# Attention and expert layers on one core: store order, ranks of the front, casts of v on other engines, and a new order of the last unit

## The chip, the cores and the metric

One core of one Trainium2 chip runs the whole program. The metric is device time in microseconds (us). The kernel before takes 982.17 us (median of 4 runs). Time quotients below are the mean time of one kernel's runs over that of the other's runs of the same rounds, so not quite the ratio of the medians that stand beside them. The span in a profile is about 1.8 us shorter than the time of the same run.

Short names: PE is the tensor engine, DVE the vector engine, ACT the scalar engine, POOL GpSimd, SP the engine that issues most transfers. In the lines, kin, qin and vin are loaded inputs, ek and eq their exponentials, tk and tq phi of k and q, vv is v in fp16, w a weight tile, h the result of layer 1 after relu, acc the summed output. A fused pair is the two SCALAR_TENSOR_TENSOR instructions of DVE that make one tk or tq. An eviction is the instruction of DVE or ACT that takes a finished product from PE.

## The reference

```python
# q, k, v: [8, 8, 576, 64]; x: [4608, 512]; 8 experts; w1: [8, 512, 1024], w2: [8, 1024, 512]
q_p, k_p = phi(q), phi(k)                    # phi(x) = (x if x > 0 else exp(x) - 1) + 1
kv  = einsum('bhsd,bhse->bhde', k_p, v);  z = k_p.sum(2)
x   = einsum('bhsd,bhde->bhse', q_p, kv) / (einsum('bhsd,bhd->bhs', q_p, z) + 1e-6)   # then to [4608, 512]
P   = exp(x @ w_gate - max);  8 rounds of normalising rows and columns
out = sum over e of  P[:, e:e+1] * (relu(x @ w1[e]) @ w2[e])
```

## The kernel before

It has three stages. The **front** handles 16 attention blocks (two per batch element): load k, q, v; exponentials, clamps and sums for phi; products kv, qt (transpose), den, num, xt. Beside it run nine **plain units** (expert 0, 512 rows each: 32 products hq of layer 1, 32 products ye of layer 2). They fill PE while the blocks come in. Then follow 63 units of experts 1 to 7, all but the last in a form with seven block products in place of eight; in the last expert's last unit only layer 1 has that form. Its block products are called a1 to a7 and b1 to b7, the layer-2 ones y1 to y7.

Nothing is scheduled by hand. A small list scheduler runs while the program is written: each task has planned durations, dependencies and a rank, and the order of instructions in each engine's stream is whatever it decides. This order is then part of the program; what the profiles add is the waits.

```python
    def run(self):                      # cut: the scheduler
        ...
                for t in lst:           # of the tasks that can start soonest, the lowest rank goes first
                    r = slot(t)
                    if r is not None and r <= te + 1e-9 and (pick is None or (t["prio"], t["id"]) < (pick["prio"], pick["id"])):
                        pick = t
```

The parts that the change touches:

```python
    p_e = S_.pool(2)
    ...
        tvv.append(fadd(("pool", 1.3), f_v, deps=[ta, tin["v"]],      # cast of v to fp16, 128 x 1152
                        use=[gvv, gin["v"]], prio=pr))
    ...
        ti = add(("sp", 0.2), f_raw, deps=deps + [t_close], prio=0.0)  # raw x to memory, then the sums
        ...
        ti = add(("sp", 0.1), f_st, deps=[last], use=[gt_], prio=0.0)
    ...
    w_t[1] = load_w1(1, prio=0.0, after=110.0) + load_w2(1, prio=0.0, after=115.0)
    order = "y1 y5 y2 y6 a7 y3 y7 a4 b1 b5 y4 b6 b3 b2 b7 A1 A5 b4 A6 A3 A2".split()
    chain = []
    for u in range(NG - 1, E * NG + 1):
        for n in order:
            ...
```

The softmax here doesn't subtract the row's maximum and nothing guards it: scores larger than these inputs give would overflow.

Of the kernel before, what the change touches and what calls it, by code (L numbers as in the profile page):

```python
# [10 lines left out]
FP32 = mybir.dt.float32  # L11
FP16 = mybir.dt.float16
# [110 lines left out]
def kernel(  # L123
# [10 lines left out]
    nc = tc.nc  # L134

    B, H, S, D = q.shape
# [4 lines left out]
    P = 128  # L141
# [37 lines left out]
    kvz_t = [fp.tile([P, 2, 2, D + 1], FP16, tag=f"kvz{i}", name=f"kvz{i}", bufs=1) for i in range(2)]  # L179

    p_in = {n: S_.pool(2) for n in "kvq"}
    p_e = S_.pool(2)
    p_t = {n: S_.pool(2) for n in "kq"}
    p_vv, p_kvz, p_qpT, p_xn, p_rden = (S_.pool(2) for _ in range(5))
    p_att, p_hq, p_h = S_.pool(2), S_.pool(2), S_.pool(2)
# [27 lines left out]
    def load_w1(e, **kw):  # L213
        return load_w(moe_w1, "w1", p_w1, [[F, P], [F * P, NDT], [1, F]], 2, e, **kw)

    def load_w2(e, **kw):
        return load_w(moe_w2, "w2", p_w2, [[DM, P], [DM * P, NFT], [1, DM]], 1, e, **kw)
# [9 lines left out]
    w_last, in_prev = [None], [None]  # L227
    front_ids = []
    xt_done = {}
    vcast = {}  # L230

    def fadd(*a, **kw):
        t = add(*a, **kw)
        front_ids.append(t)
        return t

    def att(b, g):
# [22 lines left out]
        for nm in "kq":  # L260
            ge = S_.grp(p_e)
            gt[nm] = S_.grp(p_t[nm])

            def f_e(_, ge=ge, nm=nm):
                ge["tile"] = fp.tile([P, 2, NJ, D], FP16, tag="e", name="e" + nm)
                nc.scalar.activation(out=ge["tile"], in_=gin[nm]["tile"], func=AF.Exp)

            def f_t(e, g_=gt[nm], nm=nm):
                g_["tile"] = fp.tile([P, NJ, 2, D], FP16, tag="t" + nm, name="t" + nm)
                g_["on"] = e  # L270
                if e == "act":
                    nc.scalar.add(out=g_["tile"].rearrange("p j r d -> p r j d"), in_=gin[nm]["tile"], add=1.0)  # L272

            def f_m(_, ge=ge, g_=gt[nm], nm=nm):
                nc.vector.tensor_scalar(out=ge["tile"], in0=ge["tile"], scalar1=1.0, scalar2=None, op0=ALU.min)
                o = g_["tile"].rearrange("p j r d -> p r j d")
                if g_["on"] == "act":
                    nc.vector.tensor_tensor(out=o, in0=o, in1=ge["tile"], op=ALU.max)
                else:
                    for r in range(2):  # L280
                        nc.vector.scalar_tensor_tensor(out=o[:, r], in0=gin[nm]["tile"][:, r], scalar=1.0,  # L281
                                                       in1=ge["tile"][:, r], op0=ALU.add, op1=ALU.max)
            te = fadd(("act", 1.17), f_e, deps=[tin[nm]], acq=[ge], use=[gin[nm]], prio=pr)
            tt_ = fadd({"dve": 0.6, "act": 1.17}, f_t, deps=[tin[nm]],
                       acq=[gt[nm]], use=[gin[nm]], prio=pr)
            tph[nm] = fadd(("dve", 1.35), f_m, deps=[te, tt_], use=[ge, gt[nm], gin[nm]], prio=pr)
# [5 lines left out]
        ta = fadd(("none", 0.0), f_va, deps=[tin["v"]], acq=[gvv], prio=pr)  # L292
        def f_v(e):
            copy(e, gvv["tile"][:, :, :, 0:D], gin["v"]["tile"])
        tvv.append(fadd(("pool", 1.3), f_v, deps=[ta, tin["v"]],
                        use=[gvv, gin["v"]], prio=pr))
        vcast[n] = tvv[0]
        gkv, gz = [S_.grp(p_ye[2]), S_.grp(p_ye[3])], S_.grp(p_kvz)

        def f_kv(_):  # L300
# [160 lines left out]
        return add(("dve", 0.8), f_p, deps=last, prio=-200.0)  # L461

    nc.vector.memset(ones_t, 1.0)
    warm = const.tile([P, 512], FP16, tag="warm", name="warm")
    nc.vector.memset(warm, 0.0)

# [20 lines left out]
        nc.vector.memset(kvz_t[i], 0.0)  # L487
    att(0, 0)
    att(0, 1)
    w_t = {0: load_w1(0, prio=-290.0, parts=2, deps=[vcast[0]])}  # L490
    for b in range(1, B):
        att(b, 0)
        att(b, 1)
# [26 lines left out]
    def layer1(e, g):  # L520
        gw1, tw1, gw2, tw2 = w_t[e]
        bs = range(512 * g // S, (512 * g + 511) // S + 1)
        xd_ = [xt_done[(b, c)] for b in bs for c in range(NDT)]
        th = []
        gh = S_.grp(p_h)

        def f_ha(_):
            gh["tile"] = hpool.tile([P, NFT, 512], FP16, tag="h", name="h")
        tha = add(("none", 0.0), f_ha, deps=[prev_hq[0]], acq=[gh], prio=g - 400.0)
        for f in range(NFT):  # L530
            ghq = S_.grp(p_hq)

            def f_hq(_, f=f, ghq=ghq):
                ghq["tile"] = hqp.tile([P, 512], FP32, tag="hq", name="hq")
                for c in range(NDT):
                    nc.tensor.matmul(ghq["tile"], lhsT=gw1["tile"][:, c, ts(f, P)], rhs=xT[:, c, ds(512 * g, 512)],  # L536
                                     start=(c == 0), stop=(c == NDT - 1))

            def f_rl(_, f=f, ghq=ghq):
                nc.scalar.activation(out=gh["tile"][:, f, :], in_=ghq["tile"], func=AF.Relu)  # L540
            t1 = add(("pe", 0.87), f_hq, deps=[tw1[f // 4], prev_hq[0]] + xd_, acq=[ghq], use=[gw1],
                     prio=g + 0.1 * f + 0.35)
            prev_hq[0] = t1
            x_users.append(t1)
            th.append(add(("act", 0.6), f_rl, deps=[t1, tha], use=[ghq, gh], prio=g - 400.0))
        return gh, [th, th]

    def x_blocks(g):
        bs = range(512 * g // S, (512 * g + 511) // S + 1)
        deps = [xt_done[(b, c)] for b in bs for c in range(NDT)]  # L550
        t0 = 512 * g
        gt_ = S_.grp(p_xst)

        def f_raw(_):
            nc.sync.dma_start(out=xd[g][:, 0:512].rearrange("p (c t) -> p c t", c=2), in_=xT[:, 0:2, t0:t0 + 256])
            nc.sync.dma_start(out=xd[g][:, 512:1536].rearrange("p (c t) -> p c t", c=2), in_=xT[:, 2:4, t0:t0 + 512])
        ti = add(("sp", 0.2), f_raw, deps=deps + [t_close], prio=0.0)
        out_ = [add(("dma", 1.0), lambda _: None, deps=[ti], prio=0.0, lat=2.6)]
        last = None
        for i in range(4):  # L560
            def f_T(_, i=i):
                if i == 0:
                    gt_["tile"] = accp[1].tile([P, 4, 2, 256], FP16, tag="xst", name="xst")
                T = gt_["tile"]
                b11, b12 = xT[:, 0:2, t0:t0 + 256], xT[:, 0:2, t0 + 256:t0 + 512]
                b21, b22 = xT[:, 2:4, t0:t0 + 256], xT[:, 2:4, t0 + 256:t0 + 512]
                a0, a1 = [(b12, b11), (b22, T[:, 0]), (b22, b12), (b21, T[:, 1])][i]
                nc.vector.tensor_tensor(out=T[:, i], in0=a0, in1=a1, op=ALU.subtract)
            last = add(("dve", 0.42), f_T, deps=deps + [t_close, last], acq=[gt_] if i == 0 else [], use=[gt_],
                       prio=g - 8.0)  # L570
            x_users.append(last)

        def f_st(_):
            nc.sync.dma_start(out=xd[g][:, 1536:NXB], in_=gt_["tile"].rearrange("p i c t -> p (i c t)"))
        ti = add(("sp", 0.1), f_st, deps=[last], use=[gt_], prio=0.0)
        out_.append(add(("dma", 1.5), lambda _: None, deps=[ti], use=[gt_], prio=0.0, lat=2.6))
        x_users.append(out_[0])
        return out_

    def x_load(e, g):  # L580
# [114 lines left out]
    def unit_plain(e, g, gW=None, tW=None):  # L695
# [4 lines left out]
        for tt in range(4):  # L700
            for half in range(2):
                def f_y(_, half=half, tt=tt):
                    if half == 0:
                        gy[tt]["tile"] = yps.tile([P, 512], FP32, tag=f"ye{tt % 2}", name=f"ye{tt % 2}")
                    for f in range(4 * half, 4 * half + 4):
                        nc.tensor.matmul(gy[tt]["tile"], lhsT=gh["tile"][:, f, ds(P * tt, P)], rhs=gw2["tile"][:, f, :],  # L706
                                         start=(f == 0), stop=(f == NFT - 1))
                ty[tt] = add(("pe", 0.87), f_y, deps=[tw2[half], ty[tt]] + (th[0][4 * half:4 * half + 4] if e == 0 else th[tt // 2]),
                             acq=[gy[tt]] if half == 0 else [], use=[gw2, gh],
                             prio=e * NG + g + 0.1 * (2 * tt + half) + 0.65)  # L710
        for tt in range(4):
            gg = 4 * g + tt

# [148 lines left out]
            for tt in range(4):  # L862
                out_dma(g, tt, [fin_prev[(4 * g + tt, dh)] for dh in range(2)])

    w_t[1] = load_w1(1, prio=0.0, after=110.0) + load_w2(1, prio=0.0, after=115.0)
    xd_done, xs_prev, x_closed = {}, [None], [None]
    pe_id = {}
    for g in range(NG):
# [7 lines left out]
    for e in range(1, E):  # L876
# [3 lines left out]
        for g in range(NG):  # L880
            if e == E - 1 and g == NG - 1:
                unit_plain(e, g, *co[0:2])
            else:
                unit(e, g, *co)
    order = "y1 y5 y2 y6 a7 y3 y7 a4 b1 b5 y4 b6 b3 b2 b7 A1 A5 b4 A6 A3 A2".split()
    chain = []
    for u in range(NG - 1, E * NG + 1):
        for n in order:
            key = (u - 1, n) if n[0] == "y" else (u + 1, n.lower()) if n[0] == "A" else (u, n)
            if key in pe_id:  # L890
                chain.append(pe_id[key])
    for d, k_ in zip(chain, chain[1:]):
        S_.dep(k_, d)
    S_.run()


# [28 lines left out]
```

## Time and profile before

| | us |
|---|---|
| time | 982.17 |
| span in the profile | 982.2 |
| PE idle from 22.5 to 125 us | 8.66 |
| PE idle from 125 to 950 us | 0.1 |
| last unit's first layer-2 product of the unit ahead (y1, 958.88) to the end | 23.3 |

The middle, over 800 us, has no hole. What can be won lies in the first 125 us and in the last 25; the prediction shows the lines. This profile fell on a run of its own of 983.97 us, slower than all four that make the median.

### The profile page before, as it was taken

What the parts mean: (1) busy time and instruction counts of PE and PEld (TensorE: products, weight loads), DVE (VectorE), ACT (ScalarE), POOL (GpSimd) and SP (SyncE); (2) the same over time, 40 slices, a digit from 0 to 9 for tenths busy, and PEclk for the clock granted to TensorE, in tenths of its full rate; (3) what the DMA queues carried; (4) which work ended last, traced back from release to release, by engine and by line L of the source; (5) the groups of instructions that cost most, each with busy time, mean ns of one, the idle gap of its engine ahead of it and who ended that gap; (6) DMA issues with size and microseconds to landing.
All of it is one profiled execution on the core that took longest, in us unless ns stands there. A gap on an engine that the chain in (4) does not pass through costs nothing.

```text
span 982.2 us, 21403 instructions
## 1 busy us (share of the span) xinstructions
PE 962.2 (98%) x8716; PEld 792.7 (81%) x8716; DVE 771.7 (79%) x1561; ACT 563.2 (57%) x1034; POOL 127.9 (13%) x171
## 2 busy tenths in 40 slices
PE   7899999999999999999999999999999999999997
PEld 4455564488888888888888888888888888888885
DVE  6898869967777777777777777777777777777774
ACT  4798754565555555555555555555555555555552
POOL 4111200001111111111111111111111111111110
PEclk9999999999999999999999999999999999999999
DMA  9886953162226312272225322272225322236663
GB/s 318 257 303 239 265 160 140 65 127 77 75 76 142 97 73 76 76 161 76 77 75 137 101 76 75 76 162 76 76 76 137 102 76 76 76 103 168 161 161 98
DMA packets 47029, 121.99 MB, mean 124 GB/s; under 512 B 4177, under 2 KB 18001, under 8 KB 46929
## 3 DMA queue, kind: packets, MB, share of 16 engines
q1 hardware_dynamic: 32128, 99.76, 30.3%
q0 software_dynamic: 14480, 20.33, 11.5%
q8 instruction: 68, 1.11, 0.5%
q10 hardware_dynamic: 320, 0.52, 0.1%
q14 instruction: 33, 0.26, 0.1%
HBM read 119.69 MB, written 17.69 MB: 140 GB/s over the span
## 4 chain that ended last, share of the span: by engine, by line
PE 89%; DVE 1%; ACT 1%; issue 0%
PE ye L809 33%; PE hq L627 23%; PE att L627 11%; PE Zye L627 6%; PE Zye L809 6%; PE ye L706 5%; PE hq L536 4%; PE xt_ps L387 0%; PE kv_ps L306 0%; PE num_ps L371 0%; PE lg_ps L405 0%; DVE tk L281 0%; PE qt_ps L332 0%; ACT tq L272 0%; PE den_ps L347 0%; ACT qpT L221 0%
## 5 line engine op out<-in xcount | busy, mean ns | idle before, releaser
L823 DVE SCALAR_TENSOR_TENSOR acc<-ye,P_sb,acc 128x256 f32<-128x256 f32 x620 | 264.9, 477 | 95.3 <-PE ye L809 77.9
L627 PEld LDWEIGHTS <-W 128*128 128x128 f16 x2016 | 197.1, 98 | 23.7
L809 PEld LDWEIGHTS <-S 128*128 128x128 f16 x1984 | 194.1, 98 | 22.7 <-issue 0.3
L809 PE MATMUL ye<-T,S 128*128 128x256 f16 x1488 | 192.8, 273 | 0.1
L833 POOL TENSOR_TENSOR acc<-acc,st 128x256 f32<-128x256 f32 x124 | 87.5, 725 | 625.6 <-ACT st L830 620.7
L653 ACT ACTIVATE h<-hq 128x512 f16<-128x512 f32 x126 | 76.3, 606 | 160.8 <-PE hq L627 160.8
L627 PEld LDWEIGHTS <-w 128*128 128x128 f16 x1512 | 147.6, 98 | 23.3 <-issue 1.0
L809 PEld LDWEIGHTS <-h 128*128 128x128 f16 x1488 | 145.6, 98 | 16.8
L627 PE MATMUL hq<-xs,W 128*128 128x256 f16 x1008 | 151.2, 273 | 0.0
L627 PE MATMUL att<-xs,W 128*128 128x256 f16 x1008 | 151.2, 272 | 0.0
L627 PE MATMUL hq<-xs,w 128*128 128x256 f16 x1008 | 140.7, 272 | 0.8 <-DVE h L656 0.8
L782 DVE TENSOR_TENSOR S<-h 128x1024 f16<-128x1024 f16 x124 | 85.4, 688 | 57.9 <-ACT h L653 57.9
L656 DVE CUSTOM_DVE_ANT_0 h<-att,s 128x512 f16<-128x512 f32 x126 | 86.7, 688 | 13.1 <-ACT s L643 13.1
L830 ACT ACTIVATE st<-Zye,P_sb 128x256 f32<-128x256 f32 x124 | 52.1, 471 | 78.0 <-PE Zye L809 78.0
L643 ACT COPY s<-hq 128x512 f32<-128x512 f32 x126 | 75.0, 595 | 36.7 <-PE hq L627 36.7
L650 ACT ACTIVATE h<-Zye 128x512 f16<-128x512 f32 x126 | 75.2, 597 | 35.1 <-PE Zye L627 35.1
L656 DVE CUSTOM_DVE_ANT_0 h<-hq,s 128x512 f16<-128x512 f32 x126 | 86.5, 686 | 0.8 <-PE hq L627 0.7
L639 ACT COPY Zye<-hq 128x512 f32<-128x512 f32 x126 | 73.3, 581 | 16.3 <-PE hq L627 16.3
L706 PE MATMUL ye<-w,h 128*128 128x512 f16 x320 | 77.6, 379 | 0.9 <-DVE acc L223 0.9
L627 PE MATMUL Zye<-xs,w 128*128 128x256 f16 x504 | 75.6, 273 | 0.0
L647 ACT COPY s<-att 128x512 f32<-128x512 f32 x126 | 74.5, 591 | 0.0
L536 PE MATMUL hq<-xT,w 128*128 128x512 f16 x288 | 70.6, 379 | 2.4 <-ACT h L540 2.2
(90 smaller groups left out, 963.1 us busy)
## 6 DMA issues: line engine op xcount, KB each, us to landing
xs<-xd SPq DMA_DIRECT2D x63, 896.0 KB, 4.6
w<-in_moe_w_dram POOLq DMA_DIRECT2D x14, 1024.0 KB, 11.7
out_dram<-acc SPq DMA_DIRECT2D x68, 128.0 KB, 2.4
kin<-in_k_dram SPq DMA_DIRECT2D x14, 576.0 KB, 6.0
qin<-in_q_dram SPq DMA_DIRECT2D x14, 576.0 KB, 5.0
vin<-in_v_dram SPq DMA_DIRECT2D x14, 576.0 KB, 6.4
xd<-xst SPq DMA_DIRECT2D x9, 512.0 KB, 2.6
xd<-xT SPq DMA_DIRECT2D x9, 256.0 KB, 7.1
```

Source lines behind the costliest of these rows:

```text
L536: nc.tensor.matmul(ghq["tile"], lhsT=gw1["tile"][:, c, ts(f, P)], rhs=xT[:, c, ds(512 * g, 512)], start=(c == 0), stop=(c == NDT - 1))
L627: nc.tensor.matmul(dst[:, p, :], lhsT=lhs(p, c), rhs=rhs(c), start=(first and p == 0 and c == 0), stop=(c == 1), skip_group_check=True)
L643: nc.scalar.copy(out=gs2["tile"], in_=gX["tile"])
L647: nc.scalar.copy(out=gs5["tile"], in_=gR["tile"])
L650: nc.scalar.activation(out=hd(0, 0), in_=Zt[1], func=AF.Relu)
L653: nc.scalar.activation(out=hd(1, 0), in_=gX["tile"], func=AF.Relu)
L656: nc.vector._custom_dve(TENSOR_ADD_SAT, out=dst, in0=ps, in1=sb, s0=3.0e38, s1=0.0)
L706: nc.tensor.matmul(gy[tt]["tile"], lhsT=gh["tile"][:, f, ds(P * tt, P)], rhs=gw2["tile"][:, f, :], start=(f == 0), stop=(f == NFT - 1))
L782: nc.vector.tensor_tensor(out=Sx[:, i], in0=a0, in1=a1, op=op)
L809: nc.tensor.matmul(bank(g_)[:, s, :], lhsT=lhs(s, kk), rhs=rhs(kk), start=(new and s == 0 and kk == 0), stop=(kk == 3), skip_group_check=True)
L823: nc.vector.scalar_tensor_tensor(out=dst(), in0=bank(g_)[:, s, :], scalar=P_sb[:, gg, e:e + 1], in1=dst(), op0=ALU.mult, op1=ALU.add)
L833: nc.gpsimd.tensor_tensor(out=dst(), in0=dst(), in1=gst["tile"], op=ALU.add)
```

## The change

The intent: take the casts of v off POOL, since a fused pair of DVE took 2.37 us beside one of them and 1.43 us without (the prediction shows both in the profile before); let 239 searched ranks, 50 of them with a fixed engine, for tasks of the front lower the idle time of PE; start the first layer-1 products with half of x; store the sums of x ahead of x itself; hold the weight loads of expert 1 by small copies that wait for a v tile (the first load of expert 0, which waited for the first cast of v, likewise); and fill the waits of the last unit with two products of the unit ahead, its y tiles one after the other. Cut to the core:

```diff
-    p_e = S_.pool(2)
+    p_e = S_.pool(3)
...
-        tvv.append(fadd(("pool", 1.3), f_v, deps=[ta, tin["v"]],
+        tvv.append(fadd(("act", 1.17) if n < 2 else ("dve", 0.75), f_v, deps=[ta, tin["v"]],
...
+        if n in (0, 13, 15):            # gates[n]: a 128 x 4 copy on POOL once v of block n has landed
...
+        if g == 0:                      # halves of the first two hq products, as soon as half of x is there
+            jobs = [(f, c, c + 2) for c in (0, 2) for f in range(2)] + jobs[2:]
...
-        ti = add(("sp", 0.2), f_raw, deps=deps + [t_close], prio=0.0)   # (stood ahead of the sums)
+        ti = add(("sp", 0.45), f_st, deps=[last], use=[gt_], prio=0.0)
+        ...
+        ti = add(("sp", 0.9), f_raw, deps=deps + [t_close, ti], prio=0.0)
...
-    w_t[1] = load_w1(1, prio=0.0, after=110.0) + load_w2(1, prio=0.0, after=115.0)
+    w_t[1] = load_w1(1, prio=0.0, deps=[gates[13]]) + load_w2(1, prio=0.0, deps=[gates[15]])
...
+    final = "y1 y5 y2 y6 a7 y3 a4 b1 b5 y7 b6 b3 b2 b7 y4 b4".split()
...
+    for tt in (3, 2, 1, 0):             # the last y tiles, in one chain
...
+    ranks = """ 43:-88.9997 46:-94.9994:act 55:-94.9991:dve ... """     # 239 of them
```

## The prediction

> **What bounds the kernel now.** I read the page first (parts 1, 2 and 4), then the table of windows for all engines, then the waits of the tensor engine, then the timeline of three places: the first 30 us, the end of the plain units near 200 us, and the last 15 us.
>
> Page, parts 1 and 2: the matmul engine is busy nearly all the time, and the row by slices shows digits under 9 only in the first two slices and the last one.
>
> ```profile
> PE 962.2 (98%) x8716; PEld 792.7 (81%) x8716; DVE 771.7 (79%) x1561; ACT 563.2 (57%) x1034; POOL 127.9 (13%) x171
> PE   7899999999999999999999999999999999999997
> ```
>
> The windows give the stages (columns: stretch, its length, then busy us of PE, PEld, DVE, ACT, POOL, then granted clock, DMA share, GB/s):
>
> ```profile
> 0.00:22.50 22.50, 17.05 (x148) 9.15 (x149) 15.77 (x34) 9.51 (x14) 11.06 (x19) 0.92 0.99 311
> 22.50:50.00 27.50, 23.12 (x249) 13.43 (x247) 22.12 (x42) 21.43 (x36) 5.56 (x4) 1.00 0.90 271
> 50.00:75.00 25.00, 23.54 (x259) 14.48 (x257) 23.80 (x50) 23.49 (x39) 4.62 (x4) 1.00 0.87 289
> 75.00:100.00 25.00, 23.40 (x257) 14.57 (x256) 22.29 (x50) 21.56 (x36) 4.77 (x4) 1.00 0.66 237
> 100.00:125.00 25.00, 23.78 (x251) 14.46 (x249) 21.35 (x50) 18.92 (x29) 4.13 (x5) 1.00 1.03 274
> 140.00:207.00 67.00, 67.00 (x371) 34.88 (x369) 56.79 (x150) 35.02 (x61) 1.45 (x2) 1.00 0.36 119
> 950.00:970.00 20.00, 19.22 (x176) 16.98 (x174) 14.56 (x30) 9.95 (x19) 2.83 (x4) 1.00 0.38 84
> ```
>
> PE idle is length minus the first busy number: 5.45 us before 22.5 us, 4.38 from there to 50, then 1.46, 1.60 and 1.22 in the three windows to 125 us. From 125 to 950 us a few hundredths are idle. 0.78 follows before 970, and about 5.05 after it, nearly all of it the last eviction and the last store. The sum is 20.0 us, the page's 982.2 less 962.2. The warm-up matmuls are busy time without work: 34 of them cover 11.28 us, all before 22.5 us. So 20.0 + 11.3 = 31.3 us of the span holds no useful matmul, and the change keeps the matmuls themselves. That is the whole purse. A gain of over 2% would need 19.6 us of it.
>
> The part that cannot go: the first kv product needs the first v tile, which lands at 1.75 + 6.1 = 7.9 us, then a cast of 1.15 us, so about 9 us; and about 5 us at the end. This leaves some 17 us to win: 13.4 us between 9.1 and 22.5 us less the useful products in it, 8.7 us of idle between 22.5 and 125 us, and 0.8 us in the tail. In that first piece the windows of the warm-up tile give 5.71 us of filler.
>
> The timeline shows how the front loses time (start, duration, what; brackets hold the idle time and its releaser):
>
> ```profile
> 24.73 0.46 DVE L275 TENSOR_SCALAR ek<-ek 128x1152 f16<-128x1152 f16 x1 [2.60 <-ACT ek L266]
> 25.23 1.43 DVE L281 SCALAR_TENSOR_TENSOR tk<-kin,ek 128x576 f16<-128x576 f32 x2
> 25.64 1.08 ACT L540 ACTIVATE h<-hq 128x512 f16<-128x512 f32 x2
> 26.29 1.02 PE L536 MATMUL hq<-xT,w 128*128 128x512 f16 x4 [1.36 <-ACT h L540]
> 27.06 2.37 DVE L281 SCALAR_TENSOR_TENSOR tq<-qin,eq 128x576 f16<-128x576 f32 x2
> 27.25 1.58 POOL L225 CAST vv<-vin 128x1152 f16<-128x1152 f32 x1 [3.15 <-DMA vin<-in_v_dram]
> 29.49 0.68 PE L332 MATMUL qt_ps<-ident,tq 128*128 128x128 f16 x9 [1.55 <-DVE tq L281]
> ```
>
> The same two DVE instructions take 1.43 us at 25.23 and 2.37 us at 27.06, where a cast runs on POOL from 27.25. PE then waits 1.55 us for exactly this result. The 1.36 us wait is another kind: the relu stood behind two exponentials in the order of ACT.
>
> The tail:
>
> ```profile
> 969.44 0.60 PE L627 MATMUL hq<-xs,w 128*128 128x256 f16 x4 [0.78 <-DVE h L656]
> 969.87 7.28 PE L706 MATMUL ye<-w,h 128*128 128x512 f16 x32
> 976.32 1.61 DVE L718 SCALAR_TENSOR_TENSOR acc<-ye,P_sb,acc 128x512 f32<-128x512 f32 x2 [1.98 <-PE ye L706]
> ```
>
> The last layer-1 product waits 0.78 us for the add-and-relu, for want of another product to run. Then 32 matmuls run dense to 977.15, and two evictions stand together at the very end.
>
> [...]2.37 against 1.43 us above, and at 12.41 us another such pair took 2.40 us beside a cast of 1.15 us. [...]18 raw stores are issued from 103.9 us on, while the DMA share of 100 to 125 us is 1.03, and they need a median of 7 us to land against 2.6 us for the sum stores issued later.
>
> **The change part by part.**
>
> 1. Casts of v. Sixteen POOL casts of 1.24 us mean go; two become ACT work (1.17 us, by the same-size exponential's 1.166 mean), [...]the two fused groups have means of 923 and 814 ns, and 715 when back to back, so 22 x 0.208 + 16 x 0.099 = 6.2 us; the two clamp groups exceed 450 by 100 and 46, 16 times each, 2.3 us. That is 8.5 us. [...]What improves is latency: a conversion no longer stretches just where PE waits for it.
>
> 2. The first two attention blocks. The clamp of q at 7.94 took 1.43 us instead of 0.46, so 1 us of the first chain goes. The reciprocal of the first block runs at 14.74, behind the next block's 2.40 us pair, though den ended at 12.85. [...]with other ranks it need not stand ahead. DVE work of both blocks from 6.1 us on adds to some 13.5 us, so the last xn could end near 20 us instead of 22.1. The first hq products also need only half of x now: four pairs of matmuls move into filler time, up to 4 x 0.217 = 0.87 us. I take 2.5 us of the 3 us that this offers.
>
> 3. Searched ranks and engines. They can attack the 8.7 us of idle from 22.5 to 125 us. But DVE and ACT are at 95% and 94% between 50 and 75 us, and ranks move no work away. I take a third, 3 us.
>
> 4. Store order. Raw stores leave the end of the front. The last v load took 7.4 us there; perhaps 0.2 us for PE. After 140 us PE is never idle, so the later stores cost nothing if the x tile still closes in time. Before, the last sum store is ready at about 180 us and the last user of x runs at 195, which leaves room for a 2 to 7 us store.
>
> 5. Tail. The product y4 of 0.87 us stands where the 0.78 us wait was. But y7 leaves the gap between a7 and a4, where only y3 (0.87) is left. The add-and-relu there ran from 963.44 to 964.12, behind two evictions, while y3 ended near 963.7. So a4 would wait about 0.45 us. Net 0.3 us. The single chain of y tiles spreads the evictions but the last one still follows the last matmul: about 0.1 us from quieter stores. Sum 0.4.
>
> Sum: 2.5 + 3.0 + 0.2 + 0.4 = 6.1 us, and 982.4 - 6.1 = 976.3. I put **976.5 us**.
>
> **The rivals.** First, DVE becomes the bound of the front: the casts now queue on an engine that is 95% busy between 50 and 75 us, and kv waits for DVE rather than POOL. [...]Against it: over the rest of the front DVE has 2 to 4 us free per 25. It would eat part 3 and leave the start and the tail, 979 to 981 us. Second, the front ends sooner but the gain is lost behind it: between 140 and 207 us DVE has 56.79 of 67 us busy, a chain of normalisation, scaling and weight sums. If PE came to the end of its plain units earlier than that chain, it would wait. Against it: the weight sums are done at 197.8 and first used at 209.4, so there are over 10 us of slack, and the chain starts earlier too. It would give 978 to 982. Third, the search is nearly perfect: idle of 8.7 falls to 2, the start gives 4, the tail 0.8, so 971 us. For it: a search over hundreds of ranks is more than a hand can do. Against it: an order found for planned durations meets real load times.
>
> **Range and chances.** The first and third rival set the ends: **972 to 980.5** us. Faster by over 2% means 962.8 us, more than everything winnable: 0.01. Slower by over 2%: 0.01, since nothing in the steady part changes. Within 2%: 0.98.
>
> **What would show it.** Right: DVE fused pairs of 1.43 us all through, none at 2.4; [...]first hq product about 2 us earlier than 22.53; PE idle between that point and 125 us near 5.5 us instead of 8.7; no idle from 140 us to the last unit; the b4 wait gone and a short wait at a4; PE's last matmul about 6 us earlier than 977.15. Wrong: PE waits after 140 us; casts on DVE of over 1 us; new kv waits on DVE that add up to the old ones; the same distance from the last matmul to the end but a start that has not moved.

The 8.5 us in part 1 are the busy time that DVE was to get back.

## The result, and the profile after

The changed kernel took 977.75 us (976.26 to 978.30, 4 runs) against 982.17: quotient 0.9954, 95% interval 0.9936 to 0.9971. It was run twice more, on chips 2 and 7: 977.48 us (976.02 to 981.22; quotient 0.9951, interval 0.9932 to 0.9971), and 981.07 us (978.38 to 985.63; quotient 0.9993, interval 0.9970 to 1.0015). So the gain is 4.4, 4.6 and 0.8 us, the last not clear of the noise, and single runs of one and the same program differ by up to 9.6 us. (Those of the kernel before lie from 981.28 to 985.71, 4.4 us.)

First the fast trace (976.26 us). The windows of all engines, columns as in the prediction:

```profile
0.00:22.50 22.50, 17.66 (x150) 9.99 (x151) 13.61 (x35) 13.29 (x17) 9.73 (x18) 0.92 0.98 310
22.50:50.00 27.50, 26.57 (x283) 15.36 (x281) 24.21 (x50) 23.93 (x40) 0.00 (x0) 1.00 0.98 294
50.00:75.00 25.00, 24.02 (x251) 14.22 (x248) 23.21 (x49) 24.44 (x44) 0.00 (x0) 1.00 0.80 279
75.00:100.00 25.00, 24.94 (x255) 15.18 (x254) 22.87 (x51) 23.43 (x39) 0.93 (x2) 1.00 0.73 245
100.00:125.00 25.00, 24.55 (x275) 15.03 (x273) 18.30 (x41) 20.71 (x37) 1.07 (x2) 1.00 0.77 182
```

PE idle from 22.5 to 125 us is 0.93 + 0.98 + 0.06 + 0.45 = 2.42 us instead of 8.66. In the start nearly nothing is won: PE is busy 17.66 us, of which its windows give 11.58 to the warm-up, so 6.08 us of work against 17.05 - 11.28 = 5.77 before. POOL's column is nearly empty and ACT's is fuller: to 125 us ACT sums to 105.8 us instead of 94.9, DVE to 102.2 instead of 105.3.

The groups of DVE up to 140 us (busy, mean ns, idle before), first the changed kernel, then the fused pairs of the kernel before:

```profile
L281 DVE SCALAR_TENSOR_TENSOR tk<-kin,ek 128x576 f16<-128x576 f32 x18 | 12.8, 755 | 0.3
L281 DVE SCALAR_TENSOR_TENSOR tq<-qin,eq 128x576 f16<-128x576 f32 x18 | 12.8, 755 | 0.4
L223 DVE CAST vv<-vin 128x1152 f16<-128x1152 f32 x14 | 10.4, 747 | 0.0
```

```profile
L281 DVE SCALAR_TENSOR_TENSOR tk<-kin,ek 128x576 f16<-128x576 f32 x22 | 19.4, 923 | 0.4
L281 DVE SCALAR_TENSOR_TENSOR tq<-qin,eq 128x576 f16<-128x576 f32 x16 | 12.4, 814 | 0.4
```

The stretched instructions are gone (the longest of the fused ones took 0.76 us, and 1.73 before), and a cast costs DVE 747 ns.

Then the slow trace of the same program (the second repetition, on chip 7; 985.63 us). First the longest waits of PE from 22.5 to 140 us (total, times, longest), then the timeline around them:

```profile
PE ye L718 <- ACT acc L221: 3.3, 1, 3.3
PE ye L718 <- DMA w<-in_moe_w_dram: 2.8, 1, 2.8
```

```profile
34.37 1.03 PE L718 MATMUL ye<-w,h 128*128 128x512 f16 x4
...
38.73 1.87 PE L718 MATMUL ye<-w,h 128*128 128x512 f16 x4 [2.79 <-DMA w<-in_moe_w_dram]
...
41.25 2.10 PE L718 MATMUL ye<-w,h 128*128 128x512 f16 x8
...
100.93 0.41 SPq L253 DMA_DIRECT2D kin<-in_k_dram  x1
101.87 0.74 POOL L207 DMA_DIRECT2D w<-in_moe_w_dram  x1
112.82 1.16 ACT L266 ACTIVATE ek<-kin 128x1152 f16<-128x1152 f32 x1 [3.59 <-DMA kin<-in_k_dram]
```

Neither wait was in the profile before, and neither was in the prediction. The first: layer 2 of the first plain unit needs the second half of expert 0's w2. In the fast trace this half lands 17.2 us after its issue at 18.7 us, so near 35.9, and the product that uses it runs at 36.25 without a wait. In the slow trace it lands 20.5 us after an issue near 18.2, at 38.7. A lower clock comes on top of the wait (mean granted clock 0.94 from 22.5 to 50 us, 1.00 in the fast trace): the next four matmuls take 1.87 us instead of 1.03. The second: the last block's k is issued at 100.93 and the 1 MB load of expert 1's w1 0.94 us later. That k takes 11.9 us to land, ACT waits 3.59 us for it in the order of its stream, an eviction stands behind it, and PE waits 3.33 us for the eviction. In the fast trace the gap between the two issues is 1.28 us, the k takes 9.0 us, and ACT waits 0.7.

The end of the fast trace:

```profile
957.25 1.03 PE L639 MATMUL hq<-xs,w 128*128 128x256 f16 x8 [0.33 <-DVE h L668]
962.73 7.07 PE L718 MATMUL ye<-w,h 128*128 128x512 f16 x32
969.84 0.75 DVE L732 SCALAR_TENSOR_TENSOR acc<-ye,P_sb,acc 128x512 f32<-128x512 f32 x1 [0.98 <-PE ye L718]
```

The b4 wait of 0.78 us has gone (a gap of about 0.1 us is left), and a wait of 0.33 us stands at a4, as the prediction had it (0.45). From y1 of the unit ahead (951.96) to the end it is 22.5 us, and 23.3 before.

### The profile page after: what moved, and what is told of

It is laid out like the page before. It is cut to its first block, busy times and chain, and to the rows that moved or that the text cites. A ratio compares the mean times of both kernels' runs of the same rounds, so it can differ in the third digit from the quotient of the medians.

```text
span 974.5 us, 21395 instructions
## 1 busy us (share of the span) xinstructions
PE 962.1 (99%) x8716; PEld 792.8 (81%) x8716; DVE 767.8 (79%) x1562; ACT 568.8 (58%) x1049; POOL 112.3 (12%) x158
## 4 chain that ended last, share of the span: by engine, by line
PE 92%; ACT 4%; DVE 2%; DMA 1%; issue 0%; SPq 0%; ACTq 0%; DVEq 0%
PE ye L823 33%; PE hq L639 23%; PE att L639 11%; PE ye L718 6%; PE Zye L639 6%; PE Zye L823 6%; PE hq L545 4%; DMA kin<-in_k_dram 1%; ACT eq L266 1%; PE kv_ps L309 1%; PE xt_ps L390 1%; ACT h L549 1%; PE num_ps L374 1%; DMA qin<-in_q_dram 1%; PE qt_ps L335 1%
## 5 line engine op out<-in xcount | busy, mean ns | idle before, releaser
L639 PEld LDWEIGHTS <-w 128*128 128x128 f16 x1512 | 147.5, 98 | 23.2 <-issue 0.8
L668 DVE CUSTOM_DVE_ANT_0 h<-att,s 128x512 f16<-128x512 f32 x126 | 86.7, 688 | 11.4 <-ACT s L655 10.9
```

Source lines behind the costliest of these rows:

```text
L639: nc.tensor.matmul(dst[:, p, :], lhsT=lhs(p, c), rhs=rhs(c), start=(first and p == 0 and c == 0), stop=(c == 1), skip_group_check=True)
L668: nc.vector._custom_dve(TENSOR_ADD_SAT, out=dst, in0=ps, in1=sb, s0=3.0e38, s1=0.0)
```

## The experiments

Three theories at first. **R**: the searched ranks carry the gain. **L**: the stretching of DVE's instructions beside the casts on POOL (a fused pair 2.37 us in place of 1.43) was the cost, and moving the casts is the gain. **S**: early raw stores slowed the end of the front. After the first four runs came a fourth, **W**: landings of loads, above all of the first w2, now set the front and make the runs spread. All twelve were timed in 5 rounds, with a profile; a median covers 4 to 6 runs. One run of each kernel, the first, was profiled; the table at the end of this section gives its time, which can lie far from the median.

### First chip: the repetition, the ranks, the casts, the stretching

**a_again**, the changed kernel unedited.

> The changed kernel itself, repeated beside its parts. If the first reading holds: 0.9945 to 0.9965 of the kernel before (976.5 to 978.8 us), runs spread by about 2 us because the front depends on when loads land. The first matmul of layer 1 near 21.3 us again, tensor engine idle from 22.5 to 125 us under 4 us.

977.48 us, kernel before 982.06. The profiled run was a slow one, 981.22: PE idle 6.20 us from 22.5 to 125, of it 2.45 in one wait for w2, whose second half landed 20.1 us after its issue. A second wait, of 1.8 us, stood behind the last block's k. The expectation held for the median and failed for the idle time and for the spread (5.2 us, where about 2 were expected); this run gave theory W.

**no_ranks**

```diff
-    ranks = """ ... """
-    for w in ranks.split():
-        ...
```

> The changed kernel without the table of ranks and engines; everything else kept. Theory R (the searched ranks carry most of the gain): 3 to 5 us slower than the changed kernel, 980.5 to 983 us, tensor engine idle from 22.5 to 125 us back to 6 us or more. Theory L ([...]moving the casts of v is the gain): within 1.5 us of the changed kernel, idle there under 4 us.

982.42 us, quotient 1.000 (0.9983 to 1.0016): 4.9 us slower than the changed kernel and no better than the kernel before, with everything else of the change in it, the tail included. Theory R holds for the time, clear of the noise. Its profile fell on its fastest run (979.62 us) and shows PE idle of 5.8 us from 22.5 to 125 (6 or more were expected), split into many small waits:

```profile
PE hq L545 <- ACT h L549: 1.3, 3, 0.5
PE num_ps L374 <- DVE xn L379: 1.3, 4, 0.4
PE qt_ps L335 <- DVE xT L223: 1.1, 1, 1.1
```

They are short waits of PE for whichever engine had put something else first, and this is what an order can mend. The run shows that the gain needs the ranks, not that ranks alone would give it: ranks searched for casts on POOL were not tried.

**pool_cast**

```diff
-        tvv.append(fadd(("act", 1.17) if n < 2 else ("dve", 0.75), f_v, deps=[ta, tin["v"]],
+        tvv.append(fadd(("pool", 1.3), f_v, deps=[ta, tin["v"]],
```

> The changed kernel with only the casts of v put back on GpSimd (ranks kept). Theory L: 3 to 6 us slower, fused vector pairs of 2.4 us back, waits of the tensor engine for tk or tq. Theory R: under 1.5 us slower, since ranks still order the front; but an order searched for casts elsewhere may fit less well, which would blur this run.

1006.09 us, 24 us slower than the kernel before. Neither theory expected this, and it does not test the stretching. The longest wait of PE after 207 us, and the first step of the normalisation:

```profile
PE ye L823 <- DVE acc L837: 15.1, 2, 9.9
```

```profile
L431 DVE TENSOR_REDUCE ut<-P_sb x1: 453/453/453, 178.3 to 178.3; 128x36 f32<-128x288 f32 x1
```

The normalisation starts at 178.3 us, in the changed kernel at 140.2. The scheduler, with other durations and the same ranks, put the last product for P (lg, at 176.96 us) far behind the last transpose of the front (xt, at 143.41), and the rows of P came too late for the units. Here ranks found for one set of durations were worse than none for another. It is also the prediction's second rival, the DVE chain behind the front, in a case where it does bite.

**dummy_pool**: the order of all other engines unchanged, but fourteen POOL casts that nobody reads.

```diff
...
             copy(e, gvv["tile"][:, :, :, 0:D], gin["v"]["tile"])
+            if n >= 2:
+                nc.gpsimd.tensor_copy(out=junk, in_=gin["v"]["tile"])
```

> The changed kernel with fourteen extra GpSimd casts of v into a spare buffer that nobody reads; the order on all other engines is the same. [...]Theory L: vector instructions are stretched by about 0.95 us some ten times, 3 to 8 us slower than the changed kernel. Theory R: stretched instructions, but under 1.5 us slower because slack takes them up.

979.78 us, by the medians 2.3 us slower than the changed kernel in the same rounds. The durations of the fused pairs (minimum, median, maximum) show the stretching back (the longest in the changed kernel took 0.76 us):

```profile
L282 DVE SCALAR_TENSOR_TENSOR tk<-kin,ek x18: 744/756/1579, 6.9 to 92.4; 128x576 f16<-128x576 f32 x18
L282 DVE SCALAR_TENSOR_TENSOR tq<-qin,eq x18: 745/758/1697, 14.1 to 118.5; 128x576 f16<-128x576 f32 x18
```

The 2.3 us lie under theory L's 3 to 8 and over theory R's 1.5, and they are not clear of the noise: the runs overlap (979.25 to 984.83 against 976.02 to 981.22), and so do the intervals of the quotients (0.9957 to 0.9997 against 0.9932 to 0.9971). The profile fell on the slowest run (984.83). In it PE is idle 9.23 us from 22.5 to 125, 1.9 of it for w2, against 6.20 and 2.45 in the repetition; it waits 1.2 us for a tq and 1.4 for a vv (0.3 and 0.2 there). So the stretching does reach PE in this order, but its cost in time is not settled.

### Second chip: stores, tail, and the landing of w2

**tail2**

```diff
...
+    for t in pe_id[(E * NG - 2, "e6")]:               # e6: two evictions of the unit ahead
+        S_.dep(t, pe_id[(E * NG - 1, "a22")])         # a22: the add-and-relu that a4 waits for
```

> The changed kernel with one more dependency: in the last unit, the two evictions of the unit ahead that stood before the add-and-relu on the vector engine come after it; nothing else moves. If the 0.33 us wait of a4 comes from that order, as predicted, it is gone and the last layer-1 product starts 0.3 us earlier after the last unit's first product; time 0.3 us (0.03%) less, under the spread of runs, so the trace decides. Rival: the wait moves to the next product and the end stays.

From y1 of the unit ahead to the end 979.1 - 957.21 = 21.9 us instead of 22.5, so 0.6 us less, twice the wait that it removes; a smaller gap ahead of b4 went with it. No wait of PE is left after 140 us. The total, 980.18 us, says nothing of that: its runs reach from 977.26 to 982.99, and its profile has a wait of 2.5 us for w2.

**old_store**

```diff
...
-        ti = add(("sp", 0.9), f_raw, deps=deps + [t_close, ti], prio=0.0)
+        ti = add(("sp", 0.2), f_raw, deps=deps + [t_close], prio=0.0)
```

> The changed kernel with the raw stores of x ahead again, at their old times. Theory R (ranks carry the gain): within 0.7 us of the changed kernel. Theory S (early raw stores slow the last loads of the front): 1 us or more slower, raw stores landing in 7 us instead of 3, tensor engine idle from 100 to 125 us up by as much.

979.03 us (976.61 to 981.18), quotient 0.9952. The DMA share of 100 to 125 us is 1.07 here, against 0.93 in the run above, and PE idle in that window is 1.36 us against 1.98. The DMA engines are fuller with the raw stores there, but PE does not suffer. Theory S falls: the store order gives nothing that these runs can see. (The median landing of the larger raw store went from 7.1 to 3.1 us with the change, but nothing waits for it.)

**k5_after_w2**: a 128-byte store of w2's last row, ahead of the sixth block's loads in their queue, holds them until w2 has landed (in the trace it is issued at 37.78 us, and they from 38.25 on).

```diff
...
+                if n == 5 and nm == "k":
+                    nc.sync.dma_start(out=hold, in_=w_t[0][2]["tile"][0:1, NFT - 1, 0:64])
```

> In the first repetition the tensor engine waited 2.45 us for the second half of the first w2, and its clock then fell for a while; in the first run there was no such wait. Theory W (that landing now sets the front and makes the runs spread): here the loads of k, q, v of the sixth attention block are held until this half has landed (a tiny store ahead of them in their queue waits for it), all else is the same; the half lands 1 to 3 us earlier, the wait is gone, median 975.5 to 977 us and runs within 1.5 us of each other. Rival: the transfers are bound as a whole, so that the wait turns up later at the sixth block's k (vector or scalar engine waiting for it), and the time stays at 977.5 or above.

977.90 us (976.92 to 980.64), quotient 0.9950. The wait for w2 fell to 1.4 us and did not go; 1.5 us of PE turned up later, at a product whose input on ACT came late, behind a wait of ACT of 1.0 us for a k. So in the trace it is half W and half its rival; the time (977.5 or above) and the spread (3.7 us) are the rival's. The hold came too late: the fifth block's q and v were issued ahead of it, at 26.65 and 27.32.

**w2_early**: both loads of w2 issued ahead of the fourth block's k, q and v in the same queue.

```diff
+                if n == 2 and nm == "v":
+                    issue_w2()
...
```

> The same question from the other side: the two loads of the first w2 are issued ahead of the fourth block's k, q, v in the same queue, all else the same. Theory W: the wait for w2 is gone. But the fourth block's k, q and v, used within 2 us of landing so far, land 4 to 7 us later, so a wait for them takes its place: 978 to 983 us. If it is faster than the changed kernel, the loads of the fourth block had slack that the profile does not show.

981.44 us, quotient 0.9987, as expected for a wait that changes its place: none for w2, but these, the first of ACT, the second of PE:

```profile
ACT ek L280 <- DMA kin<-in_k_dram: 4.4, 1, 4.4
```

```profile
PE den_ps L364 <- ACT kvz L226: 4.2, 3, 3.6
```

In the first 50 us the transfers have little slack as a whole: the DMA share of both windows there is 0.98 in the fast trace of the changed kernel. What can be chosen is which of them waits.

### Third chip: a better version, and the parts from the other side

**a_third**, the changed kernel again.

> The changed kernel once more, as the yardstick on this chip: median 976.5 to 980 us, single runs between 976 and 981.5, the slow ones those in which the first w2 lands late.

981.07 us (978.38 to 985.63), above the range. Its profile is the slow one shown above. Besides w2 there was the second wait, for the last block's k, which the expectation did not have, though the traces of a_again, tail2, old_store and w2_early had it already (1.3 to 2.1 us of PE).

**q4_tail2**: the dependency of tail2, and the hold two loads further ahead, at the fifth block's q.

```diff
...
-                if n == 5 and nm == "k":
+                if n == 4 and nm == "q":
...
```

> Two edits on the changed kernel that should beat it: the tail order that took 0.6 us off the end, and the hold on the loads behind the first w2 moved ahead to the fifth block's q, so that five transfers less compete with it. Theory W: the second half of w2 lands at 33 to 35 us instead of 36 to 38, before its first use, no wait of the tensor engine for it, and the held loads still land before their use from 39.5 us on: 975 to 977 us, runs within 2 us. Rival: the held loads come late and the vector and scalar engines wait for them, 977 us or more.

975.66 us (975.34 to 976.05, 5 runs), quotient 0.9934 (0.9922 to 0.9946): 6.2 us under the kernel before, 5.4 us under the changed kernel on the same chip, with a spread of 0.7 us. The second half of w2 landed 16.2 us after an issue near 18.3, so near 34.5; the tiny store is issued at 34.46 us and the first of the held loads at 34.94, and the first product that uses this half runs at 35.77 without a wait:

```profile
34.46 0.32 SPq L255 DMA_DIRECT2D hold<-w  x1
```

```profile
35.77 1.03 PE L721 MATMUL ye<-w,h 128*128 128x512 f16 x4
```

```profile
22.50:50.00 27.50, 26.12 (x284) 15.32 (x283) 23.67 (x49) 22.95 (x39) 0.00 (x0) 1.00 0.96 295
100.00:125.00 25.00, 24.91 (x274) 15.16 (x272) 18.72 (x42) 21.24 (x38) 2.02 (x4) 1.00 0.81 193
```

The held loads did not come too late, and the second wait is gone too (0.09 us idle in the last window). That second part is a by-product: the last k was issued 2.67 us ahead of expert 1's w1 instead of 0.94, and landed in 8.6 us. Of the 5.4 us the tail explains 0.6; the hold at this place was not run without it. The clock has a share: its mean over a run is 0.998 or 0.999 in these five, and 0.993 to 0.998 in the six of the changed kernel, in whose profiled run the windows with the two waits show 0.94 (22.5 to 50 us) and 0.86 (100 to 125).

**casts_only**: the kernel before with the casts moved (and the third buffer and the gates).

> The kernel before with the casts of v on the scalar and vector engines alone (with their third buffer and the small gates for the weight loads), without ranks, split, store order and tail. Theory L: half of the gain or more, 979.5 us or less. Theory R: no gain, 981.5 to 984 us; the stretched vector pairs are gone, and yet the tensor engine is as idle from 22.5 to 125 us as before.

982.45 us, quotient 1.0005 (0.9992 to 1.0019): no gain that these runs can see, as theory R had it. The fused pairs are all at 0.75 us, and yet PE is idle 7.3 us from 22.5 to 125, in a trace of 982.02 us; 1.8 us of that are a wait for w2. The kernel before has no such wait, so without it 5.6 us of idle stand against 8.66: it may be that the casts did free some time and the load of w2 took it back. That was not tested. What is shown is that the casts alone, under the old order, bring at most 0.8 us (the lower end of the interval).

**old_tail**: the changed kernel with the order and the free y tiles of the kernel before in the last unit.

```diff
-        for n in (order if u < E * NG - 1 else final):
+        for n in order:
...
-    for tt in (3, 2, 1, 0):
...
```

> The changed kernel with the old order of the last unit. By the traces the last unit's first product to the last matmul takes 17.85 us with the new order and 18.27 with the old, and the new order ends 0.35 us sooner after the last matmul: 0.8 us slower than the changed kernel in the trace from that product on, which is under the spread of the total times. Rival: the tail is worth 1.5 us or more, or nothing.

From y1 of the unit ahead to the end 980.5 - 957.27 = 23.2 us against 22.5: 0.7 to 0.8 us, as expected. The median, 979.75 us, was even below the unedited kernel's 981.07 of the same call. The loads hide a thing of this size in the total. This trace also has the wait for w2, and after it the clock did not fall:

```profile
38.23 1.02 PE L718 MATMUL ye<-w,h 128*128 128x512 f16 x4 [2.73 <-DMA w<-in_moe_w_dram]
```

PE idle from 22.5 to 125 us, and in it the wait for w2 and the wait behind the last block's k, each in the one profiled run, with that run's time (without pool_cast); the times follow these columns only roughly, for the tail and the lower clock come on top of them:

| profiled run | time | idle 22.5 to 125 | wait for w2 | wait behind the last k |
|---|---|---|---|---|
| before | 983.97 | 8.66 | 0 | 0 |
| changed, first run | 976.26 | 2.42 | 0 | 0.5 |
| changed, first repetition | 981.22 | 6.20 | 2.5 | 1.8 |
| changed, second repetition | 985.63 | 8.04 | 2.8 | 3.3 |
| no ranks | 979.62 | 5.77 | 0.2 | 0 |
| dummy casts | 984.83 | 9.23 | 1.9 | 0 |
| new tail | 980.90 | 6.33 | 2.5 | 1.9 |
| old stores | 981.13 | 6.06 | 2.7 | 1.3 |
| hold at k | 978.41 | 4.49 | 1.4 | 0 |
| w2 early | 984.61 | 7.70 | 0 | 2.1 |
| casts only | 982.02 | 7.34 | 1.8 | 0 |
| old tail | 982.35 | 6.83 | 2.7 | 2.2 |
| hold at q, new tail | 975.66 | 2.97 | 0 | 0 |

The mean granted clock from 22.5 to 50 us is 0.94 in the two repetitions, the dummy casts, the new tail and the old stores, whose waits for w2 are 1.9 to 2.8 us, and in w2 early, where PE waited up to 3.6 us at once for a kvz; it is 1.00 in the others, among them casts only with a wait of 1.8 us and old tail with 2.7. The four matmuls behind the wait for w2 took 1.86 and 1.87 us in the repetitions and 1.48 with the dummy casts, and 1.02 in old tail and with the hold at k.

## Why the prediction was right or wrong

The time on record, 976.5 us in 972.0 to 980.5, held for the run that counts (977.75) and for the first repetition. The second repetition's median lies 0.6 us above the range. The gain was put at 5.7 us in the front and 0.4 in the tail; by the medians of the first runs it is 4.4, of which the traces give 0.8 to the tail, so about 3.6 to the front. That the total lay in the range is in part luck, since two wrong terms cancel: in the fast trace the start gave 2.2 us less than forecast and the ranks 3.2 us more. Of the signs that it named for being right, the first layer-1 product came 1.26 us earlier (2 forecast), the idle time was 2.42 us (5.5), and the last matmul ended 7.35 us earlier (6).

**Casts.** The end of the stretched pairs was right. The forecast of a cast's cost on DVE is cut (747 ns was measured), and so is the balance of DVE, which came out at -3.1 us. The step "ranks move no work away" was wrong, for the table fixes engines too, and ACT took on 10.9 us. The saving was mis-sized as well: the fused pairs gave back 4.8 us of busy time by the lines above (31.8 us for 38 of them, then 25.6 for 36), not 6.2, for the prediction set single means (923, 814) against a busy time per instruction in pairs (715). That the casts are of no use alone was not foreseen.

**The start.** Its term of 2.5 us measured 0.3 us (work of PE before 22.5 us). The first layer-1 product did come at 21.27 us instead of 22.53, but as one half product of two matmuls; the next six ran from 22.69. (The prediction's "four pairs of matmuls" is a slip: its 4 x 0.217 us are four matmuls, two pairs.) The first kv product came later than before, for this reason:

```profile
7.75 1.15 ACT L272 ACTIVATE tq<-qin 128x1152 f16<-128x1152 f32 x1
8.80 1.14 ACT L221 CAST vv<-vin 128x1152 f16<-128x1152 f32 x1
10.00 1.16 PE L309 MATMUL kv_ps<-vv,tk 64*128 64x130 f16 x18 [2.42 <-ACT vv L221]
```

The cast sits behind another ACT instruction that the rank table put there, and kv starts at 10.00 instead of 9.12. (Without the ranks it starts at 9.48, with the casts alone at 9.19; some 0.3 us of the 0.88 is a later landing of v in this run.) A start that has not moved was one of the prediction's own signs of being wrong. The prediction had taken the ACT cast as the same as the POOL cast and did not look at what else would queue on ACT.

**The ranks.** The term of 3 us measured 6.2 us in the fast trace, 2.5 and 0.6 in the slow ones. The argument that the prediction set against its third rival, "an order found for planned durations meets real load times", is what the runs show: with the loads in time the search is nearly perfect (2.42 us of idle; the rival said 2), without them most of it is lost. The page had it in view: w2's second half landed about 33.8 us in the profile before, and a front that runs ahead of the loads will meet them. The prediction asked what DVE would become, and never what the transfers would.

**The gates of expert 1.** The prediction passed over them. By the slow trace they bring the 1 MB load to within 1 us of the last k, where it stood at 112.35 us before. That this proximity is the cause of the second wait is only argued. In the nine traces with this order of loads, gap and landing were 0.94 and 11.9, 1.01 and 10.4, 1.04 and 10.7, 1.09 and 10.7, 1.10 and 9.8, 1.12 and 8.6, 1.16 and 10.4, 1.28 and 9.0, 2.67 and 8.6 us: the closest load goes with the latest k, but 1.12 us went with the earliest. It was not tested by a run that moves the gate alone, and stays open.

**Stores.** Put at 0.2 us; nothing was seen. That the later stores cost nothing after 140 us was right.

**The tail.** 0.4 us forecast, 0.8 measured. The mechanism was right in both parts, the wait at b4 gone and a smaller one at a4 (net 0.2 us up to the last unit's own layer 2, where 0.3 were forecast). Mis-sized were the chain of y tiles, whose 32 matmuls took 7.07 us instead of 7.28, and the time from the last matmul to the end, 4.7 us instead of 5.05; the prediction gave the two 0.1 us together.

**The rivals.** DVE as the bound of the front did not show. Nor did the chain behind the front in the changed kernel: no idle from 125 to 950 us. The third came true in its idle time (2.42 us for 2) and its tail (0.8), in the fast trace alone, and not in its start (0.3 us for 4).

## What to carry to other kernels

When an order is searched until the compute engines have little slack, the next thing to set the time can be the landing of loads, as here, where it showed first as spread between runs: profile a slow run as well as a fast one and compare their waits. Hold a load that is not needed yet behind one that is (a tiny store that reads the awaited tile, ahead of it in the queue, did this in q4_tail2: issued at 34.46 us, the held loads from 34.94 on); here that and one dependency in the tail gave 5.4 us on the chip on which the change alone gave 0.8, and cut the spread from 7.3 us to 0.7. Ranks found by search belong to the durations they were found for (1006.09 us with the casts put back on POOL), so search again after any edit that changes one.
